# The last batch of a two-lane mixer kernel in 64-row halves, and the lower lane's products for u moved eight places later

## The chip, the cores and the metric

The kernel runs on one core of a Trainium2 chip. The metric is the device time of one execution in microseconds; of several runs the median counts. The arithmetic is float32 in the reference; the kernel carries each operand as a rounded float32r part ("hi") and the rest ("lo"), and multiplies the parts that matter.

## The reference

```python
def _attn_ref(x, weight_gen):          # x: 8 x 4096 x 192, weight_gen: 8 x 4096 x 8 heads x 7 taps
    w = softmax(weight_gen, axis=-1)
    ...                                # causal: seven rows of x, each head's 24 columns weighted by w
    return einsum('bshk,bskhg->bshg', w, x_unf).reshape(B, S, D)

def _moe_ref(x, w_tok1, w_tok2, w_ch1, w_ch2):
    xt = x.transpose(0, 2, 1)
    h = np.maximum(xt @ w_tok1, 0.0) @ w_tok2      # over the 4096 places: 4096 -> 256 -> 4096
    u = x + h.transpose(0, 2, 1)
    h2 = np.maximum(u @ w_ch1, 0.0) @ w_ch2        # over the 192 channels: 192 -> 1536 -> 192
    return u + h2
```

`reference` is `_moe_ref(_attn_ref(x, weight_gen), ...)`.

## The kernel before

Work goes by chunks of 512 places: eight batches of eight chunks, 64 chunks `g` = 0 to 63. Of each chunk the core computes:

- the attention sums (VectorE products `pr`, L278 and L292, summed into `xa` partly by accumulating DMAs of GpSimd), which run some eight chunks ahead,
- `token1`: 16 products per half into the bank pair `th`, which hold the running sum of a batch; ScalarE seeds the banks with the sum so far (`w<-h1s`, L609) and takes it out again (`h1s<-w`, L637),
- `token2`: u = x + h of the next chunk in the bank pair `up`; ScalarE seeds it with x (`w<-xb`, L664), then come ten products of 128 rows (six for bank 0, four for bank 1), or ten per half; `uf` takes it out (L683, L684, L688). Then `u_parts` (L691 to L728) makes `u_hi` and `u_lo`, the operands of the next chunk, in places that suit both halves: eight copies on ScalarE and two subtractions on VectorE,
- `channel1`: six blocks `p`, each of nine products per half into a tile `ph` of two banks (54 products per half), with `take_h` behind each block: ScalarE's relu (L799) and VectorE's rest (L800) into `h`; for blocks 4 and 5 in two steps each into `h_spare` (L792, L793),
- `channel2`: 60 products of 128 rows, or 60 per half, into the bank pair `acc`, which ScalarE seeds with u (L878); `store` turns the result (L887, L888 on VectorE), copies it to `out_tile` (L897 on ScalarE, twelve copies) and sends it out.

**Two ways to run a chunk.** In the plain way TensorE's products of `token2` and `channel2` take 128 rows of the array, and those of `channel1` come in pairs of 64 rows. `in_lanes` (L1558) says which chunks run in lanes instead: 16 to 54. There `chunk_in_lanes` (L1398) gives every product as two of 64 rows, the upper half (lane 0) and the lower half (lane 1). The two lanes work through their lists in different order, so that one lane can be in `channel2` while the other is in `token2` or `token1`. Two halves must not write one bank at once: a bank belongs to one lane until that lane's products for it are done; then a relay (a `nop` on VectorE or ScalarE, whichever the planner thinks is free earlier, L1389) hands it over.

**What sets the order.** The order is made when the program is written. A planner inside the kernel keeps estimated times of the engines (`at`, `on`), of the lanes (`lane_at`) and a cost per product (`SLOT`, 226.7 ns), and always writes down the product of the lane that would start first (`run_lanes`, L1370). Each engine then runs its queue in that order, TensorE one queue for both lanes. Other ScalarE and VectorE work (attention, stores, u's parts) is fitted in by `pump`.

**The lists of a chunk in lanes** are in `section` (L1463): `a` is `channel2` for bank 0 (36 products per lane), `c` the one for bank 1 (24), `u` is `token2` (ten); `la`, `lc`, `lu` are the lower lane's. `early` and `late` are `token1`'s products; a chunk in lanes has the late ones, the first chunk has both. The upper lane runs a, u, c, then token1; the lower lane runs part of `lc`, then `lu`, the rest of `lc`, token1, `la`:

```python
upper = a + u + [hook(end_two), *c, late[0], hook(lambda: end_one("late"))]
lower = lc[:4] + lu + lc[4:14] + [hook(lambda: seed_late(1))] + lc[14:] + [late[1]] + la
```

`hook` marks a place where something is written down without a product: `end_two` the taking out of u and its parts, `seed_late` the seed of `th`. Three tiles of two banks (`ring`) serve `ph`, `up` and `th` in turn; block 3's `ph` gets the tile of block 0, `up` the one of block 3.

Of the kernel before, what the change touches and what calls it, by code (L numbers as in the profile page):

```python
# [22 lines left out]
def mixer_kernel(ctx: ExitStack, tc: tile.TileContext, x, wg, wt1, wt2, wc1, wc2, out):  # L23
# [629 lines left out]
    def token2(m, up=None, lists=None):  # L653
# [28 lines left out]
        if seeded:  # L682
            nc.scalar.copy(u[c, 1, :], up[e, 1, :])  # L683
            nc.scalar.copy(u[:, 0, :], up[:, 0, :])  # L684
        else:
            nc.vector.tensor_add(u[:, 0, :], up[:, 0, :], xb[:, 0, :])
            nc.vector.tensor_add(u[c, 1, :], up[e, 1, :], xb[e, 1, :])
        nc.vector.tensor_add(u[c, 1, :], up[c, 1, :], u[c, 1, :])  # L688

    def u_parts(m):  # L690
# [37 lines left out]
        return first(), second()  # L728

# [313 lines left out]
    HANDOVER = 60  # L1043
# [312 lines left out]
    def lane_start(s):  # L1356

        while lanes[s] and lanes[s][0][0] == 0:
            at["pe"] = max(at["pe"], lane_at[s]) if s == 0 else at["pe"]
            lanes[s].popleft()[2]()  # L1360
        if not lanes[s]:
            return None
        bank, t = lanes[s][0][1], lane_at[s]
        if bank in owner and owner[bank] != s:
            if bank not in turn:
                return None
            t = max(t, turn[bank][1] + HANDOVER)
        return t

    def run_lanes(until):  # L1370

        while True:
# [7 lines left out]
            if bank is not None:  # L1380
# [4 lines left out]
                else:  # L1385
                    count[bank] = count.get(bank, 0) + 1
                    if count[bank] == ITEMS[bank[:2]]:
                        by, eng = min((("dve", nc.vector), ("act", nc.scalar)), key=lambda x: at[x[0]])
                        relay = eng.nop(nofuse=True)  # L1389
                        behind(relay, ins)  # L1390
                        turn[bank] = relay, on(by, 60, lane_at[s] + HOP)
# [7 lines left out]
    def chunk_in_lanes(g):  # L1399
# [4 lines left out]
        twice = max(state["token1"], state["open"]) < g + NCH  # L1404
# [62 lines left out]
        def section():  # L1467
# [5 lines left out]
            if "early" in box:  # L1473
                early = [hook(lambda s=s: open_one("early", s)) for s in range(2)]
                upper = [early[0]] + a + u + [hook(end_two)] + c + [late[0]]
                lower = lc[:8] + [early[1], hook(lambda: end_one("early"))] + lu + lc[8:] + la \
                    + [hook(finish), late[1], hook(lambda: end_one("late"))]
            elif box["late"]:
                upper = a + u + [hook(end_two), *c, late[0], hook(lambda: end_one("late"))]
                lower = lc[:4] + lu + lc[4:14] + [hook(lambda: seed_late(1))] + lc[14:] + [late[1]] + la  # L1480
            else:
                upper = a + u + [hook(end_two)] + c
                lower = lc[:4] + lu + lc[4:] + la
# [36 lines left out]
        def end_two():  # L1520
# [3 lines left out]
            t = max(on("dve", 690, on("act", 620, t)), on("act", 620))  # L1524
            w_at.append(t)
            chains[3:3] = [Chain(items, t, ("u", m)) for items in u_parts(m)]
# [31 lines left out]
    def in_lanes(g):  # L1558

        return 2 * NCH <= g < NG - NCH - 1 and (ring or state["token1"] >= g + NCH - 1 and state["done"] > g + NCH)  # L1560
# [124 lines left out]
```

## Time and profile before

| | |
|---|---|
| median of three runs | 2068.48 us (2068.37 to 2068.87) |
| the profiled execution's own time | 2068.67 us |
| its span, first to last instruction | 2066.9 us |
| PE, PEld busy | 2033.7 us (98%), 1737.9 us (84%) |
| DVE, ACT busy | 1501.7 us (73%), 1449.3 us (70%) |
| granted TensorE clock | 1.00 of 2.4 GHz, mean of the span |

PE is TensorE's products, PEld its weight loads, which run beside them; DVE is VectorE, ACT is ScalarE, ACTq and DVEq are their queues' own steps. A product's record lasts longer than the step from one product to the next, because products are pipelined: busy time says little on the steps, starts say more. "64*128" in an instruction's form is a product on half of the array's rows. In lanes two products start in each step of about 0.227 us. The name `w` in rows of chunks in lanes is any tile of the ring: `w<-u_hi,w_hi` is `channel1`, `w<-w,h` is `token2`, `w<-xh,w` is `token1`. Until chunk 15 the program runs the plain way, to about 586 us; then lanes to 1805 us; then the plain way again.

### The profile page before, as it was taken

The numbers are of one execution on the slowest core, as the hardware profiler recorded it, in microseconds if no ns is written. First come the engines' busy times: TensorE is split into PE (matmuls) and PEld (weight loads), VectorE is DVE, ScalarE is ACT, GpSimd is POOL, SyncE is SP. The second block draws the span as 40 slices with busy tenths as digits, with TensorE's granted clock in tenths as the row PEclk, the third lists the DMA queues.
The fourth block names the chain that finished last, engine by engine and source line by source line (L and its number), as shares of the span: only waits on it lengthen the run. The fifth ranks groups of instructions, "written<-read, shape, count | busy, mean of one in ns | idle before, by whom it ended". The sixth has DMA issues, their size and how long they took to land.

```text
span 2066.9 us, 39312 instructions
## 1 busy us (share of the span) xinstructions
PE 2033.7 (98%) x16201; PEld 1737.9 (84%) x16201; DVE 1501.7 (73%) x1813; ACT 1449.3 (70%) x2360; POOL 210.6 (10%) x292
## 2 busy tenths in 40 slices
PE   7999999999999999999999999999999999999999
PEld 7878888888888888888888888888888889888887
DVE  9899888888987768777778777768778774343343
ACT  7887667677766676776766677667677667676665
POOL 1101111111111101101101110101100110000000
PEclk9999999999999999999999999999999999999999
DMA  9878778787886766766767666666666663222121
GB/s 337 276 228 230 198 210 230 210 237 199 231 220 174 194 173 167 192 180 171 191 160 197 182 169 185 176 174 190 179 172 181 173 160 117 72 68 62 51 64 24
DMA packets 180928, 361.93 MB, mean 175 GB/s; under 512 B 26138, under 2 KB 129178, under 8 KB 165004
## 3 DMA queue, kind: packets, MB, share of 16 engines
q1 hardware_dynamic: 145420, 225.35, 35.4%
q0 software_dynamic: 35328, 134.07, 27.8%
q8 instruction: 127, 2.08, 0.4%
q14 instruction: 53, 0.43, 0.1%
HBM read 222.77 MB, written 70.52 MB: 142 GB/s over the span
## 4 chain that ended last, share of the span: by engine, by line
PE 79%; DVE 14%; ACT 5%; issue 2%; ACTq 0%; DMA 0%; DVEq 0%
PE acc L469 22%; PE w L469 21%; PE acc L811 15%; PE ph L782 10%; DVE h L800 5%; PE w L782 5%; DVE pr L278 2%; PE up L676 2%; ACT h L799 2%; ACT w L664 2%; PE th L648 2%; DVE pr L292 1%; DVE prk L404 1%; DVE h_spare L793 1%; PE w L676 1%
## 5 line engine op out<-in xcount | busy, mean ns | idle before, releaser
L469 PE MATMUL acc<-h,w2s 64*128 64x512 f32 x3120 | 556.5, 388 | 0.0
L469 PEld LDWEIGHTS acc<-h,w2s 64*128 64x128 f32 x3120 | 441.3, 184 | 34.6
L469 PE MATMUL w<-u_hi,w_hi 64*128 64x512 f32 x1404 | 370.9, 389 | 0.0
L469 PE MATMUL w<-u_hi,w_lo 64*128 64x512 f32 x1404 | 368.7, 387 | 0.0
L469 PE MATMUL w<-u_lo,w_hi 64*128 64x512 f32 x1404 | 368.4, 386 | 0.0
L469 PE MATMUL acc<-h_spare,w2s 64*128 64x512 f32 x1560 | 335.6, 386 | 0.0
L811 PE MATMUL acc<-h,w2s 128*128 128x512 f32 x1400 | 325.6, 390 | 0.0
L799 ACT ACTIVATE h<-w 128x1024 fp32r<-128x1024 f32 x210 | 215.6, 1027 | 148.7 <-PE w L469 80.8
L278 DVE TENSOR_TENSOR pr<-xc,wg 128x768 f32<-128x768 f32 x336 | 313.0, 945 | 0.2
L811 PEld LDWEIGHTS acc<-h,w2s 128*128 128x128 f32 x1400 | 261.8, 188 | 54.4 <-issue 0.7
L800 DVE SCALAR_TENSOR_TENSOR h<-w,h 128x1024 fp32r<-128x1024 f32 x210 | 255.7, 1218 | 71.0 <-ACT h L799 70.5
L296 POOL DMA_DIRECT2D xa<-pr x168 | 146.7, 873 | 1374.2 <-DVE pr L292 1002.2
L469 PEld LDWEIGHTS acc<-h_spare,w2s 64*128 64x128 f32 x1560 | 258.4, 184 | 23.4
L469 PEld LDWEIGHTS w<-u_hi,w_hi 64*128 64x128 f32 x1404 | 250.8, 184 | 24.1 <-DVE h L800 2.9
L469 PEld LDWEIGHTS w<-u_hi,w_lo 64*128 64x128 f32 x1404 | 253.8, 184 | 20.0
L469 PEld LDWEIGHTS w<-u_lo,w_hi 64*128 64x128 f32 x1404 | 254.9, 184 | 17.0
L688 DVE TENSOR_TENSOR uf<-w,uf 64x512 f32<-64x512 f32 x47 | 32.1, 683 | 256.5 <-ACT uf L684 256.5
L897 ACT COPY out_tile<-oa 32x256 f32<-32x256 f32 x504 | 203.7, 404 | 7.6
L469 PE MATMUL w<-w,h 64*128 64x512 f32 x780 | 194.9, 393 | 11.0 <-ACT w L664 11.0
L469 PEld LDWEIGHTS w<-xh,w 64*128 64x128 f32 x1280 | 187.6, 186 | 6.6 <-ACTq L1389 0.8
L469 PE MATMUL w<-xh,w 64*128 64x384 f32 (+1 forms) x1280 | 192.2, 300 | 0.6 <-ACTq L1389 0.4
L469 PEld LDWEIGHTS w<-w,h 64*128 64x128 f32 x780 | 140.7, 184 | 40.3 <-ACT w L664 26.9
(147 smaller groups left out, 3192.3 us busy)
## 6 DMA issues: line engine op xcount, KB each, us to landing
w<-s SPq DMA_DIRECT2D x96, 1024.0 KB, 6.5
xa<-pr POOLq DMA_DIRECT2D x168, 384.0 KB, 4.9
xc<-in_x_dram POOLq DMA_DIRECT2D x42, 960.0 KB, 9.6
out_dram<-out_tile SPq DMA_DIRECT2D x128, 192.0 KB, 2.6
xb<-xs SPq DMA_DIRECT2D x348, 64.0 KB, 5.1
xs<-t SPq DMA_DIRECT2D x56, 384.0 KB, 3.3
raw<-in_moe_w_tok_dram SPq DMA_DIRECT2D x16, 1024.0 KB, 8.3
xc<-in_x_dram POOLq DMA_DIRECT2D x12, 840.0 KB, 10.5
```

What stands on the lines that cost most here:

```text
L278: nc.vector.tensor_mul(t.rearrange("p t (h g) -> p (t h) g", h=H).rearrange("p (o n) g -> p o n g", o=1), x_k, w)
L296: nc.gpsimd.dma_start(xat[m].rearrange("p t d -> p (t d)"), tap_sums[m].rearrange("p t d -> p (t d)"), accum_op=ALU.add)
L469: return lambda: nc.tensor.matmul(to, w, v, start=start, stop=stop, skip_group_check=True)
L648: nc.tensor.matmul(to, w[:, c, r * P:(r + 1) * P], xat[m][:, c, :], start=c == first, stop=c == last, skip_group_check=True)
L664: nc.scalar.copy(up.rearrange("p k (n b c) -> p (k n) c b", c=W, b=Q), xb.rearrange("p k (n c b) -> p (k n) c b", c=W, b=Q))
L676: nc.tensor.matmul(up[:, n, :], h1[:, k, d], w[:, l, k * N:(k + 1) * N], start=k == 0 and j == 0 and not seeded, stop=k == KR - 1 and j == ...
L688: nc.vector.tensor_add(u[c, 1, :], up[c, 1, :], u[c, 1, :])
L782: nc.tensor.matmul(ph[:, j, :], w[rows, k, p * P:(p + 1) * P], u[rows, k], start=n == 0, stop=n == len(steps) - 1)
L799: nc.scalar.activation(h[:, :, 0, :], ph, AF.Relu)
L800: nc.vector.scalar_tensor_tensor(h[:, :, 1, :], ph, 0.0, h[:, :, 0, :].bitcast(F32), op0=ALU.max, op1=ALU.subtract)
L811: nc.tensor.matmul(acc[n], w2s[:, f, d], h[:, j, l, :], start=False, stop=f == NF - 1 and i == len(steps) - 1, skip_group_check=True)
L897: nc.scalar.copy(dst, src[to:to + Q].rearrange("p (n e d) -> p n e d", n=2, d=Q)[:, n])
```

## The change

1. `in_lanes` now holds for 16 to 62, so the eight chunks 55 to 62 run in lanes too; chunk 63 stays plain. `twice` is limited so that no token1 product is asked for that doesn't exist.
2. In all three kinds of chunk in lanes the lower lane runs twelve products of `lc` before `lu`; before it was four, and eight in the first chunk in lanes. The seeds of `token1` stand at other places in the lists.
3. For u of chunks 57 to 63, `quick_parts` replaces `u_parts`: u's taking out and its parts are written down at once, in one order, five casts and one copy on ScalarE, three casts, one copy, one addition and two subtractions on VectorE. `token2` puts u's first copy on VectorE there.
4. The planner's allowance for handing a bank over is 200 ns ahead of the relay, where 60 ns stood ahead of it (`HOP`) and 60 ns behind it (`HANDOVER`).

```diff
@@ -681,7 +681,7 @@
         c, e = slice(0, DC), slice(DC, P)
         if seeded:
             nc.scalar.copy(u[c, 1, :], up[e, 1, :])
-            nc.scalar.copy(u[:, 0, :], up[:, 0, :])
+            (nc.scalar.copy if m <= NG - NCH else nc.vector.tensor_copy)(u[:, 0, :], up[:, 0, :])
         else:
             nc.vector.tensor_add(u[:, 0, :], up[:, 0, :], xb[:, 0, :])
             nc.vector.tensor_add(u[c, 1, :], up[e, 1, :], xb[e, 1, :])
@@ -726,6 +726,40 @@
             yield "u", 620, lambda: act(hi[e, 2], uc[c])
             yield "n", 0, last
         return first(), second()
+
+
+    def quick_parts(m, t):
+
+        ua, uc = uft[m][:, 0, :], uft[m][:, 1, :]
+        c, e = slice(0, DC), slice(DC, P)
+        hi, lo = ut[m] = [late.tile([P, 3, N], F32R, tag=x, name=x) for x in ("u_hi", "u_lo")]
+        f, fh = lo.bitcast(F32), hi.bitcast(F32)
+
+        def act(to, of, *after):
+            nc.scalar.copy(to, of)
+            return on("act", 620, *after)
+
+        def copy(to, of, *after):
+            nc.vector.tensor_copy(to, of)
+            return on("dve", 420, *after)
+
+        def sub(to, of, less, *after):
+            nc.vector.tensor_sub(to, of, less)
+            return on("dve", 680, *after)
+        wide, narrow = on("dve", 620, t), on("act", 620, t)
+        narrow = on("dve", 690, narrow)
+        a = act(hi[:, 0], ua, wide)
+        b = act(hi[c, 2], uc[c], narrow)
+        la = sub(lo[:, 0], ua, fh[:, 0], a)
+        copy(hi[c, 1], fh[e, 0])
+        lb = sub(lo[c, 2], uc[c], fh[c, 2], b)
+        act(hi[e, 1], fh[c, 0])
+        copy(hi[e, 2], fh[c, 2])
+        act(lo[e, 1], f[c, 0], la)
+        copy(lo[c, 1], f[e, 0])
+        act(lo[e, 2], f[c, 2], lb)
+        free["u"] = max(at["act"], at["dve"]) + HOP
+        return narrow
 
 
     ht, acc_t = {}, {}
@@ -1040,7 +1074,7 @@
     AHEAD = 2
     MOVES = 2
     LANE_TIGHT = 600
-    HANDOVER = 60
+    HANDOVER = 200
     state = {"token1": NCH - 1, "token2": -1, "vals": 0, "few": 0, "few_t": 0, "late": False, "jobs": deque(),
              "summed": NCH - 1, "turned": FT - 1, "parts": NCH - 1, "kept": FT - 1, "stored": -1, "out": -1,
              "done": NCH - 1, "w1": NCH + 1, "channel1": 0, "rest": 0, "open": 0}
@@ -1364,7 +1398,7 @@
         if bank in owner and owner[bank] != s:
             if bank not in turn:
                 return None
-            t = max(t, turn[bank][1] + HANDOVER)
+            t = max(t, turn[bank][1])
         return t
 
     def run_lanes(until):
@@ -1388,7 +1422,7 @@
                         by, eng = min((("dve", nc.vector), ("act", nc.scalar)), key=lambda x: at[x[0]])
                         relay = eng.nop(nofuse=True)
                         behind(relay, ins)
-                        turn[bank] = relay, on(by, 60, lane_at[s] + HOP)
+                        turn[bank] = relay, on(by, 60, lane_at[s] + HANDOVER)
             if s == 0:
                 at["pe"] = lane_at[0]
 
@@ -1401,7 +1435,7 @@
         top, low = lanes
         phs, box = {}, {}
         need(lambda: g in ut)
-        twice = max(state["token1"], state["open"]) < g + NCH
+        twice = max(state["token1"], state["open"]) < min(g + NCH, NG - 1)
 
         def before(p):
             phs[p] = w_tile("ph")
@@ -1472,15 +1506,15 @@
             late = [hook(lambda s=s: open_one("late", s)) for s in range(2)]
             if "early" in box:
                 early = [hook(lambda s=s: open_one("early", s)) for s in range(2)]
-                upper = [early[0]] + a + u + [hook(end_two)] + c + [late[0]]
-                lower = lc[:8] + [early[1], hook(lambda: end_one("early"))] + lu + lc[8:] + la \
+                upper = [early[0]] + a + u + [hook(end_two)] + c[:12] + [hook(lambda: seed_late(0))] + c[12:] + [late[0]]
+                lower = lc[:12] + [early[1], hook(lambda: end_one("early"))] + lu + lc[12:] + la \
                     + [hook(finish), late[1], hook(lambda: end_one("late"))]
             elif box["late"]:
                 upper = a + u + [hook(end_two), *c, late[0], hook(lambda: end_one("late"))]
-                lower = lc[:4] + lu + lc[4:14] + [hook(lambda: seed_late(1))] + lc[14:] + [late[1]] + la
+                lower = lc[:12] + lu + lc[12:16] + [hook(lambda: seed_late(1))] + lc[16:] + [late[1]] + la
             else:
                 upper = a + u + [hook(end_two)] + c
-                lower = lc[:4] + lu + lc[4:] + la
+                lower = lc[:12] + lu + lc[12:] + la
             if not twice:
                 lower.append(hook(finish))
             box["end"] = lane_at[0] + sum(x[0] for x in upper) + (twice or box["late"]) * T1
@@ -1521,9 +1555,12 @@
             m, t = g + 1, max(lane_at) + HOP
             pump(t + SLACK_M, (), t + SLACK_A)
             next(box["two"], None)
-            t = max(on("dve", 690, on("act", 620, t)), on("act", 620))
-            w_at.append(t)
-            chains[3:3] = [Chain(items, t, ("u", m)) for items in u_parts(m)]
+            if m > NG - NCH:
+                w_at.append(quick_parts(m, t))
+            else:
+                t = max(on("dve", 690, on("act", 620, t)), on("act", 620))
+                w_at.append(t)
+                chains[3:3] = [Chain(items, t, ("u", m)) for items in u_parts(m)]
             state["token2"] = m
             if m + 2 < NG:
                 add_chain(iter([("gate", 0, lambda: state["kept"] >= m + 2 + (m + 1) % 2),
@@ -1557,7 +1594,7 @@
 
     def in_lanes(g):
 
-        return 2 * NCH <= g < NG - NCH - 1 and (ring or state["token1"] >= g + NCH - 1 and state["done"] > g + NCH)
+        return 2 * NCH <= g < NG - 1 and (ring or state["token1"] >= g + NCH - 1 and state["done"] > g + NCH)
 
     for g in range(NG):
         if in_lanes(g):
```

How the order moves. First, TensorE in chunk 41, from the end of `channel1` to the first product of `token2` (`w_5980<-w2,h1`). Rows of the lower lane here are those of `acc1` and `token2`, of the upper lane those of `acc0`; the numbers of `h` rise with the block. Before:

```order
L469 MATMUL w_5982<-u_lo_15713,w1_hi_71 128x512
L469 MATMUL acc0_15917<-h_15864,w2s_73 128x512
L469 MATMUL acc1_15918<-h_15864,w2s_73 128x512
L469 MATMUL acc0_15917<-h_15889,w2s_73 128x512
L469 MATMUL acc1_15918<-h_15864,w2s_73 128x512
L469 MATMUL acc0_15917<-h_15889,w2s_73 128x512
L469 MATMUL acc1_15918<-h_15864,w2s_73 128x512
L469 MATMUL acc0_15917<-h_15889,w2s_73 128x512
L469 MATMUL acc1_15918<-h_15864,w2s_73 128x512
L469 MATMUL acc0_15917<-h_15889,w2s_73 128x512
L469 MATMUL w_5980<-w2_15714,h1_15040 128x512
```

and in the changed kernel, from the lower lane's ninth product of bank 1:

```order
L469 MATMUL acc1_15919<-h_15915,w2s_73 128x512
L469 MATMUL acc0_15918<-h_15915,w2s_73 128x512
L469 MATMUL acc1_15919<-h_15915,w2s_73 128x512
L469 MATMUL acc0_15918<-h_15915,w2s_73 128x512
L469 MATMUL acc1_15919<-h_15915,w2s_73 128x512
L469 MATMUL acc0_15918<-h_15915,w2s_73 128x512
L469 MATMUL acc1_15919<-h_15915,w2s_73 128x512
L469 MATMUL acc0_15918<-h_15942,w2s_73 128x512
L469 MATMUL w_5980<-w2_15713,h1_15040 128x512
L469 MATMUL acc0_15918<-h_15942,w2s_73 128x512
```

Before, the first product of `token2` follows four products of the lower lane in bank 1, all of block 0; now it follows twelve, the last from block 2. The upper lane has gone on to block 3 by then, and stood at block 1 before.

Second, TensorE at the end of the same chunk, where the upper lane has begun `channel1` of the next one (`u_hi`, `u_lo`) and the lower lane ends its `channel2` (`acc0<-h_spare`). Before:

```order
L469 MATMUL acc0_15917<-h_spare_5979,w2s_73 128x512
L469 MATMUL w_5982<-u_hi_16098,w1_lo_72 128x512
L469 MATMUL acc0_15917<-h_spare_5979,w2s_73 128x512
L469 MATMUL w_5982<-u_hi_16098,w1_lo_72 128x512
L469 MATMUL acc0_15917<-h_spare_5979,w2s_73 128x512
L469 MATMUL w_5982<-u_hi_16098,w1_lo_72 128x512
L469 MATMUL w_5982<-u_hi_16098,w1_hi_71 128x512
L469 MATMUL w_5982<-u_lo_16099,w1_hi_71 128x512
L469 MATMUL w_5982<-u_hi_16098,w1_hi_71 128x512
```

and now:

```order
L469 MATMUL acc0_15918<-h_spare_5979,w2s_73 128x512
L469 MATMUL w_5982<-u_hi_16097,w1_lo_72 128x512
L469 MATMUL acc0_15918<-h_spare_5979,w2s_73 128x512
L469 MATMUL w_5982<-u_hi_16097,w1_lo_72 128x512
L469 MATMUL acc0_15918<-h_spare_5979,w2s_73 128x512
L469 MATMUL w_5982<-u_lo_16098,w1_hi_71 128x512
L469 MATMUL w_5982<-u_hi_16097,w1_hi_71 128x512
L469 MATMUL w_5982<-u_lo_16098,w1_hi_71 128x512
L469 MATMUL w_5982<-u_hi_16097,w1_hi_71 128x512
```

Behind the last row of `acc0` comes one more product of the upper lane, its sixth of the block before (`w1_lo`) and its seventh now (`u_lo`), and then the lower lane's first of `channel1`. The lower lane stands one product further behind the upper one, in this and the other chunks of the middle batches.

Third, VectorE in the last batch, for one u (of chunk 60 or so), from the relu's rest of the chunk to the next `store`. Before:

```order
L890 TENSOR_TENSOR oc<-oc 64x512
L800 SCALAR_TENSOR_TENSOR h<-w,h 128x2x512 x4
L688 TENSOR_TENSOR uf<-w,uf 64x512
L800 SCALAR_TENSOR_TENSOR h<-w,h 128x2x512
L714 TENSOR_TENSOR u_lo<-uf,u_hi 128x512
L715 TENSOR_TENSOR u_lo<-uf,u_hi 64x512
L800 SCALAR_TENSOR_TENSOR h<-w,h 128x2x512
L887 STREAM_TRANSPOSE oa<-acc_22484 128x512
```

and now:

```order
L834 SCALAR_TENSOR_TENSOR h<-w,h 128x2x512 x4
L827 SCALAR_TENSOR_TENSOR h_spare<-w,h_spare 128x512 x4
L684 COPY uf<-w 128x512
L688 TENSOR_TENSOR uf<-w,uf 64x512
L747 TENSOR_TENSOR u_lo<-uf,u_hi 128x512
L743 CAST u_hi<-u_hi 64x512
L747 TENSOR_TENSOR u_lo<-uf,u_hi 64x512
L743 CAST u_hi<-u_hi 64x512
L743 CAST u_lo<-u_lo 64x512
L921 STREAM_TRANSPOSE oa<-acc_22548 128x512
L922 STREAM_TRANSPOSE oc<-acc_22549 128x512
```

Before, two `take_h` steps of the chunk stand between u's steps, and ScalarE has eight of u's ten parts; now all of `take_h` is ahead of u, and five of the ten parts and the first copy of u are VectorE's.

On ScalarE and VectorE the order of chunks 17 to 53 is the same before and after, but for a swap of neighbours on each of the two engines in the first chunk in lanes and the relays' places.

## Rows read from the trace of the kernel before

**Rows 1.** Busy times of chunk 53: us, PE, PEld, DVE, ACT, POOL, clock, DMA.
```profile
1743.20:1773.90 30.70, 30.70 (x284) 27.33 (x282) 12.53 (x15) 21.50 (x36) 0.00 (x0) 1.00 0.31 95
```

**Rows 2.** Chain of waits, last batch: start us, us, what.
```profile
1876.26 2.51 PE w L676 x10
1878.78 13.60 PE acc L811 x60
1892.38 12.49 PE w L782 x108
```

**Rows 3.** Who TensorE waited for, whole run: total us, times, longest us.
```profile
PEld w L469 <- ACT w L664: 26.9, 38, 0.9
...
PEld w L469 <- DVE h L800: 2.9, 16, 0.2
...
PEld w L469 <- ACTq L1389: 0.8, 1, 0.8
...
PEld w L469 <- ACT w L609: 0.6, 1, 0.6
...
PE w L469 <- ACT w L664: 11.0, 35, 0.4
```

**Rows 4.** Timeline, seed and first token2 product, chunk 41: start, us, what [idle <-releaser].
```profile
1383.59 1.02 ACT L664 COPY w<-xb 128x1024 f32<-128x1024 f32 x1
...
1384.66 0.18 PEld L469 LDWEIGHTS w<-w,h 64*128 64x128 f32 x1 [0.82 <-ACT w L664]
1384.66 0.50 PE L469 MATMUL w<-w,h 64*128 64x512 f32 x1 [0.40 <-ACT w L664]
```

**Rows 5.** Timeline, the same place in chunk 54: a load, its product, token2's load.
```profile
1786.70 0.18 PEld L469 LDWEIGHTS w<-u_lo,w_hi 64*128 64x128 f32 x1
...
1786.92 0.39 PE L469 MATMUL w<-u_lo,w_hi 64*128 64x512 f32 x1
...
1788.45 0.18 PEld L469 LDWEIGHTS w<-w,h 64*128 64x128 f32 x1 [0.38 <-ACT w L664]
```

**Rows 6.** Timeline of VectorE: the turns that begin a chunk's store.
```profile
1371.10 0.72 DVE L887 STREAM_TRANSPOSE oa<-acc 128x512 f32<-128x512 f32 x1 [0.71 <-PE acc L469]
...
1433.47 0.72 DVE L887 STREAM_TRANSPOSE oa<-acc 128x512 f32<-128x512 f32 x1 [0.71 <-PE acc L469]
...
1775.33 0.72 DVE L887 STREAM_TRANSPOSE oa<-acc 128x512 f32<-128x512 f32 x1 [5.76 <-PE acc L469]
...
2035.48 0.72 DVE L887 STREAM_TRANSPOSE oa<-acc 128x512 f32<-128x512 f32 x1 [6.79 <-PE acc L811]
```

**Rows 7.** Timeline, token1's seed and first product (chunk 41); its products (chunk 54).
```profile
1389.87 0.80 ACT L609 COPY w<-h1s 128x768 f32<-128x768 f32 x1
...
1391.64 0.33 PE L469 MATMUL w<-xh,w 64*128 64x384 f32 x1
...
1795.39 0.33 PE L469 MATMUL w<-xh,w 64*128 64x384 f32 x1
...
1797.64 2.92 PE L469 MATMUL acc<-h,w2s 64*128 64x512 f32 x24
```

**Rows 8.** Timeline, a chunk with softmax steps: block 0's h, block 3's first load.
```profile
1343.35 1.21 DVE L800 SCALAR_TENSOR_TENSOR h<-w,h 128x1024 fp32r<-128x1024 f32 x1
...
1344.62 0.18 PEld L469 LDWEIGHTS w<-u_hi,w_hi 64*128 64x128 f32 x1 [0.18 <-DVE h L800]
```

**Rows 9.** Timeline, last batch: from pairs of 64 rows to products of 128.
```profile
1876.19 2.15 PEld L676 LDWEIGHTS w<-w,h 128*128 128x128 f32 x10 [0.35 <-issue]
```

**Rows 10.** Timeline of ScalarE: first and last of u's steps in chunk 41.
```profile
1393.25 0.58 ACT L683 COPY uf<-w 64x512 f32<-64x512 f32 x1 [2.58 <-PE w L469]
...
1398.99 0.62 ACT L718 CAST u_lo<-u_lo 64x512 fp32r<-64x512 f32 x1
```

**Rows 11.** A VectorE cast of 64x512, at L769: ns min/median/max, start us.
```profile
L769 DVE CAST u_lo<-u_lo x1: 421/421/421, 89.1 to 89.1; 64x512 fp32r<-64x512 f32 x1
```

**Rows 12.** Timeline of VectorE, chunk 42, behind the last take of h.
```profile
1418.39 1.81 DVE L278 TENSOR_TENSOR pr<-xc,wg 128x768 f32<-128x768 f32 x2
```

## The prediction

> **What bounds the kernel now.** I read the busy times first. TensorE's products cover all of a chunk's 30.70 us, VectorE is busy 12.53 us of it and ScalarE 21.50, and the granted clock is 1.00, the upper level of 2.4 GHz [rows 1]. So TensorE sets the time, and only idle steps of TensorE can be won; busy time hides them, since a product's record (0.39 us) is longer than the step of 0.227 us between products of one lane. The list of who waited for whom names the steps: the weight loads of lanes wait 26.9 us in 38 places for ScalarE's seed of `up`, 2.9 us in 16 places for VectorE's `h`, and twice in the first chunk in lanes [rows 3]. The chain shows the last batch: 2.51 + 13.60 + 12.49 = 28.60 us a chunk, all TensorE's [rows 2].
>
> **The wait for the seed of `up`.** In chunk 41 the seed ends at 1383.59 + 1.02 = 1384.61 and the first load of `token2` starts at 1384.66, after 0.82 us without one [rows 4]. What is lost is less: a load is normally 0.22 us ahead of its product (1786.70, 1786.92) [rows 5], whereas the late one starts with it and its product lasts 0.50 instead of 0.39, so the product comes 0.11 behind its load [rows 4]. The loss is the idle time less 0.11. Three of the 38 places (chunks 52 to 54, without attention work) idle 0.38 [rows 5], the other 35 share 26.9 - 3 x 0.38 = 25.8, or 0.736 each: (0.736 - 0.11) x 35 = 21.9 us. A second way: two chunks take 1433.47 - 1371.10 = 62.37 [rows 6], 31.18 each; chunk 53 takes 30.70 with 0.27 lost [rows 1, 5]; 31.18 - 30.43 = 0.75, of which some 0.07 is the wait for `h` (below): 0.68 x 35 = 23.8. I take 22.5. The lowest bound is TensorE's own idle record, 11.0 us [rows 3]; I don't use it, because the overlapping records hide part of each gap.
>
> The change puts eight more products of the lower lane ahead of `token2`: 8 x 0.227 = 1.81 us. In the order ScalarE and VectorE run the same steps as before in these chunks, so the seed stays where it is, 0.7 us late against a place that moves by 1.81: about 1.1 us early. The wait goes, **-22.5 us**, and in chunks 52 and 53 another 2 x 0.27 = **-0.5**.
>
> What is late next? `token1`'s seed ends at 1390.67 and its first product follows at 1391.64, 0.97 us later [rows 7]. The lower lane has 34 products ahead of it as before, so without the stall the product comes 0.72 earlier and 0.25 us is left: enough for a load 0.22 ahead. The cost is nothing, and where ScalarE were late, it would be a stall here. The steps behind `token2` (u's parts, `store`, VectorE's products) wait for TensorE and move with it.
>
> **The lower lane is one product further behind.** In 16 chunks (every second one, those with softmax steps) block 3's first load waits for VectorE's `h` of block 0: that ends at 1343.35 + 1.21 = 1344.56, the load starts at 1344.62, 0.18 late [rows 8]. VectorE's steps hang on the lower lane's end, block 3 of the upper lane doesn't; one product more between the lanes makes this load 0.227 later against its place. If both lanes lose it each time, 16 x 0.227 = 3.6 us. If the lanes slide against each other within the given order (an offset of up to one product is free, and the stall at `token2` no longer lines the lanes up again), it costs nothing. I take the middle, **+1.8**, and keep 0 and 3.6.
>
> **The first chunk in lanes** loses a load to a relay that stands behind ScalarE's `h_spare` (0.8 us) and one to `token1`'s seed (0.6) [rows 3]. The first is reached four products (0.9 us) later now, the second's seed stands three casts of 0.62 [rows 10] earlier: (0.8 - 0.11) + (0.6 - 0.11) = **-1.2**, bounds 0 and -1.2.
>
> **The last batch.** From the store of chunk 53 to that of chunk 62 it takes 2035.48 - 1775.33 = 260.15 us for nine chunks [rows 6]. It holds one start of the plain way with its waits, and in each plain chunk two changes between pairs of 64 rows and products of 128, where no load can be put ahead: 0.35 idle at one [rows 9], about 0.2 us lost. After the change chunk 54 takes 30.70 - 0.27 = 30.43. The chunks 55 to 62 do the same without `token1`, whose 16 products take 1797.64 - 1795.39 = 2.25 [rows 7]: 28.18 each, 225.4 for eight. Together 255.9; at the end of the lanes the lower one runs its last three or four products alone, about 0.4. So 256.3 against 260.15, **-3.9**.
>
> This holds if u is ready in time, for without `token1` only the upper lane's 24 products of bank 1 (5.4 us) lie between the end of `token2` and the next `channel1`. The old steps take 1398.99 + 0.62 - 1393.25 = 6.36 [rows 10]. The new ones: ScalarE one copy and five casts, 0.58 + 5 x 0.62 = 3.7; VectorE three casts at 0.42 [rows 11], an addition and two subtractions of about 0.68, and a copy of 128x512 out of the banks, which the trace doesn't show; the turn of the same size out of the banks takes 0.72 [rows 6], ScalarE's narrower copy 0.58 [rows 10], I take 0.65. That is 4.0; with the hand-overs between the two some 4.3 us, a us to spare. Chunk 55 keeps the old steps, but what ends last there is `u_lo`, six products later in use.
>
> **One rule against the change.** A load runs beside the products of both lanes: at 1786.70 a load starts, its product follows 0.22 later, and the product ahead of it is still running [rows 5]. The Trainium skill ("TensorE: Matmul & The Clock Gate", section "Part 3: Packing small matmuls — row/col tiling") says that a weight load overlaps running products only when the row group differs. By that rule a lane would pay each load of 0.18 us, in the last batch, for the 60 + 10 products of a chunk that were of 128 rows, 8 x 70 x 0.18 = 101 us more. The trace doesn't agree; the sum goes by the 30.70 of a chunk in lanes.
>
> **The sum.** -22.5 - 0.5 + 1.8 - 1.2 - 3.9 = -26.3. The profiled execution took 2068.67, so 2042.4; the median of the runs is 0.2 lower: **2042.2 us**.
>
> **Rivals.** (A) The lanes slide and block 3 waits no more: the 1.8 goes, and with it up to 2.2 of today's wait: 2038 to 2040.4. (B) `token1`'s seed takes the place: each 0.1 us over the 0.25 that is left costs 3.5 us in 35 chunks, and a late load 0.11 each. For it speaks that a relay stands ahead of the seed on ScalarE in half of these chunks; against it, that the relay's product ends 1.5 us before ScalarE gets there. 0.3 late gives (0.05 + 0.11) x 35 = 5.6, so 2048; 0.5 late 2055. (C) u is late in the last batch, as with the old steps' 6.36: about 0.9 x 7 = 6.4, 2048.6. (D) The change does not do what it says, ScalarE's seed of `up` follows `token2` and the wait stays: only the ends are won, 2068.5 - 3.9 - 0.2 = 2064.4. (E) Slower than before: the relay that hands the second bank of `up` to the upper lane now stands behind two of VectorE's products in 16 chunks, which end at 1418.39 + 1.81 = 1420.20 [rows 12]; the upper lane needs the bank 36 products after the section's start (1414.3), at 1422.5. VectorE 2.3 us late is the point from which TensorE waits, and 1.6 us more eats the 26 us: 5 us late gives 16 x 2.7 = 43, 2085. Against it: those products start without idle time here. (F) The page's rule on loads: 2042 + 101 = 2143.
>
> **How the numbers follow.** Forecast 0.60 (its own 2040.4 to 2046), A 0.13, B 0.11, C 0.08, D 0.04, E 0.03, F 0.01. A measurement of this kernel can tell some 0.2% (4 us) from no change. Faster by more: forecast, A, B, C, 0.92; within: D, 0.04; slower: E and F, 0.04. The range runs from below A, with the last of the small waits gone, to C and the half of B: 2037.5 to 2050.
>
> **What the changed profile should show.** No load waits for `w<-xb`; a chunk of the middle batches takes 30.4 to 30.6 us; loads waiting for `h` 0.2 to 0.4 in 16 places or none; the chunks 55 to 62 28.1 to 28.3 us; no load behind `w<-h1s`. A new releaser with some 35 entries would make B right; 29 us a chunk in the last batch C. The prediction is wrong in its main step if the wait for `w<-xb` stays.

## The result, and the profile after

The changed kernel takes 2041.97 us (median of four runs, 2041.88 to 2042.06) against 2068.43 (2068.24 to 2068.87) of the kernel before: a ratio of 0.9872, 95% interval 0.9855 to 0.9889, or 26.5 us less. The forecast was 2042.2. The profiled execution's span fell from 2066.9 to 2040.3 us.

From the page of the changed kernel, busy times of the whole span:

```profile
PE 2018.7 (99%) x16761; PEld 1756.4 (86%) x16761; DVE 1519.5 (74%) x1857; ACT 1436.1 (70%) x2348; POOL 210.2 (10%) x292
```

TensorE is still the bound. The list of who waited for whom in the changed kernel, the weight loads of lanes alone (total us, times, longest us), answers to [rows 3]; L834 is what was L800, L1423 what was L1389:

```profile
PEld w L469 <- DVE h L834: 7.5, 18, 0.6
...
PEld w L469 <- ACTq L1423: 0.8, 1, 0.8
...
PEld acc L469 <- DVEq L1423: 0.6, 1, 0.6
```

The 26.9 us behind ScalarE's seed of `up` are gone, and so is the 0.6 behind the seed of `token1`. The wait for VectorE's `h` has grown from 2.9 us in 16 places to 7.5 in 18 (the two new places, 0.57 and 0.28 us, lie in the first chunk in lanes), the relay of the first chunk stayed, and one wait for a relay on VectorE is new. The same places in the timeline (start us, us, what, idle before and releaser), in order of time:

```profile
1355.87 0.72 DVE L921 STREAM_TRANSPOSE oa<-acc 128x512 f32<-128x512 f32 x1 [0.73 <-PE acc L469]
...
1368.39 1.02 ACT L664 COPY w<-xb 128x1024 f32<-128x1024 f32 x1
...
1370.49 0.18 PEld L469 LDWEIGHTS w<-w,h 64*128 64x128 f32 x1
...
1389.24 0.62 DVE L240 TENSOR_REDUCE mx<-wg 128x64 f32<-128x448 f32 x1
...
1389.78 1.21 DVE L834 SCALAR_TENSOR_TENSOR h<-w,h 128x1024 fp32r<-128x1024 f32 x1
...
1391.04 0.18 PEld L469 LDWEIGHTS w<-u_hi,w_hi 64*128 64x128 f32 x1 [0.41 <-DVE h L834]
...
1417.07 0.72 DVE L921 STREAM_TRANSPOSE oa<-acc 128x512 f32<-128x512 f32 x1 [0.72 <-PE acc L469]
...
1435.87 0.80 ACT L609 COPY w<-h1s 128x768 f32<-128x768 f32 x1
...
1436.73 0.18 PEld L469 LDWEIGHTS w<-xh,w 64*128 64x128 f32 x1
...
1436.90 0.42 PE L469 MATMUL w<-xh,w 64*128 64x384 f32 x2
...
1831.73 0.18 PEld L469 LDWEIGHTS acc<-h,w2s 64*128 64x128 f32 x1 [0.56 <-DVEq L1423]
...
1896.49 0.72 DVE L921 STREAM_TRANSPOSE oa<-acc 128x512 f32<-128x512 f32 x1 [1.52 <-PE acc L469]
...
1918.34 0.58 ACT L683 COPY uf<-w 64x512 f32<-64x512 f32 x1 [3.55 <-PE w L469]
...
1922.67 0.42 DVE L743 CAST u_lo<-u_lo 64x512 fp32r<-64x512 f32 x1
...
1923.30 0.18 PEld L469 LDWEIGHTS w<-u_hi,w_hi 64*128 64x128 f32 x1
...
1924.62 0.72 DVE L921 STREAM_TRANSPOSE oa<-acc 128x512 f32<-128x512 f32 x1 [1.52 <-PE acc L469]
```

Read it by pairs. Two middle chunks take 1417.07 - 1355.87 = 61.20 us, where they took 62.37 [rows 6]. The seed of `up` ends at 1369.41 and `token2`'s first load follows 1.08 us later, without idle time. The seed of `token1` ends at 1436.67; its first load starts 0.06 later and its product at 1436.90, in step with the other lane: close behind the seed, but nothing is lost. Block 3's load waits 0.41 us for `h` (0.18 in [rows 8]), and that `h` stands behind a softmax reduction (L240) which ends after ScalarE's part. A chunk of the last batch takes 1924.62 - 1896.49 = 28.13 us, before 28.60 [rows 2].

The stores' first turns cut the run into stretches (us between turns):

| stretch, store to store | before | after | difference | forecast |
|---|---|---|---|---|
| chunk 15 to 17: first chunk in lanes, and one stall at token2 | 67.76 | 65.58 | -2.2 | -1.2 - 0.6 |
| 17 to 51: middle, with softmax steps | 1059.87 | 1040.05 | -19.8 | -21.9 + 1.8 |
| 51 to 53: middle, without | 61.40 | 60.93 | -0.5 | -0.5 |
| 53 to 62: chunk 54 and the last batch | 260.15 | 256.00 | -4.2 | -3.9 |

### The profile page after: what moved, and what is told of

The parts are those of the page before. It is cut to its first block, busy times and chain, and to the rows that moved or that the text cites. A ratio compares the mean times of both kernels' runs of the same rounds, so it can differ in the third digit from the quotient of the medians.

```text
span 2040.3 us, 40471 instructions
## 1 busy us (share of the span) xinstructions
PE 2018.7 (99%) x16761; PEld 1756.4 (86%) x16761; DVE 1519.5 (74%) x1857; ACT 1436.1 (70%) x2348; POOL 210.2 (10%) x292
## 4 chain that ended last, share of the span: by engine, by line
PE 94%; DVE 4%; ACT 1%; DMA 1%; issue 0%; ACTq 0%; DVEq 0%
PE w L469 36%; PE acc L469 33%; PE acc L845 9%; PE ph L816 9%; PE up L676 2%; PE th L648 2%; DVE prk L404 1%; PE w L816 1%; DMA out_dram<-out_tile 1%; PE up L845 1%; PE tapsum L414 1%; PE th L627 1%; DVE h L834 1%; DVE pr L278 0%; PE acc L882 0%; DVE val L202 0%
## 5 line engine op out<-in xcount | busy, mean ns | idle before, releaser
L469 PE MATMUL acc<-h,w2s 64*128 64x512 f32 x3760 | 615.6, 387 | 0.1
L469 PEld LDWEIGHTS acc<-h,w2s 64*128 64x128 f32 x3760 | 500.3, 184 | 47.2 <-DVEq L1423 0.6
L469 PE MATMUL w<-u_hi,w_hi 64*128 64x512 f32 x1692 | 441.4, 389 | 0.1
L469 PE MATMUL w<-u_hi,w_lo 64*128 64x512 f32 x1692 | 437.0, 388 | 0.0
L469 PE MATMUL w<-u_lo,w_hi 64*128 64x512 f32 x1692 | 434.7, 387 | 0.0
L469 PEld LDWEIGHTS w<-u_lo,w_hi 64*128 64x128 f32 x1692 | 306.5, 184 | 26.0
L834 DVE SCALAR_TENSOR_TENSOR h<-w,h 128x1024 fp32r<-128x1024 f32 x194 | 236.3, 1218 | 61.7 <-ACT h L833 61.1
L845 PE MATMUL acc<-h,w2s 128*128 128x512 f32 x920 | 215.6, 391 | 0.0
L826 ACT ACTIVATE h_spare<-w 128x512 fp32r<-128x512 f32 x188 | 112.5, 598 | 133.2 <-DVE h_spare L827 86.3
L845 PEld LDWEIGHTS acc<-h,w2s 128*128 128x128 f32 x920 | 171.7, 188 | 35.6 <-issue 0.4
L827 DVE SCALAR_TENSOR_TENSOR h_spare<-w,h_spare 128x512 fp32r<-128x512 f32 x188 | 129.0, 686 | 83.5 <-ACT h_spare L826 83.5
```

Of the source, the lines that this page charges most:

```text
L469: return lambda: nc.tensor.matmul(to, w, v, start=start, stop=stop, skip_group_check=True)
L826: nc.scalar.activation(h[:, 0, :], ph[:, j, :], AF.Relu)
L827: nc.vector.scalar_tensor_tensor(h[:, 1, :], ph[:, j, :], 0.0, h[:, 0, :].bitcast(F32), op0=ALU.max, op1=ALU.subtract)
L834: nc.vector.scalar_tensor_tensor(h[:, :, 1, :], ph, 0.0, h[:, :, 0, :].bitcast(F32), op0=ALU.max, op1=ALU.subtract)
L845: nc.tensor.matmul(acc[n], w2s[:, f, d], h[:, j, l, :], start=False, stop=f == NF - 1 and i == len(steps) - 1, skip_group_check=True)
```

## The experiments

Each was run beside the kernel before, and its difference is taken against the 2041.97 of the changed kernel; the kernel before took 2068.14 to 2068.82 on the chips used, so differences under about half a microsecond are not read. "Time lost" below is worked out from the traces: each product is given its undisturbed step (0.2267 us for a pair of half products of 512 columns), and what the starts fall behind at a place is added up. Such a sum over the middle chunks is good to a few tenths of a microsecond, depending on how many products around a stall are counted to it.

### How many products ahead of token2

```diff
-lower = lc[:12] + lu + lc[12:16] + [hook(lambda: seed_late(1))] + lc[16:] + [late[1]] + la
+lower = lc[:4] + lu + lc[4:14] + [hook(lambda: seed_late(1))] + lc[14:] + [late[1]] + la
```

and the same four in the list without `token1`; then six and eight (`lc[:6]`, `lc[:8]`) with the seed left at `lc[16:]`. VectorE and ScalarE run the same order in all of them.

> Four of the lower lane's products ahead of token2 again in the steady chunks and the last batch (the seeds of token1 at their old place); all else as in the changed kernel. Mine: the wait for the seed of up comes back, 35 x 0.63 = 21.9 us in chunks 17 to 51, and 0.27 in each of the 11 chunks without softmax work, 3.0: 2041.97 + 24.9 = 2066.9, with about 29 us of idle loads behind ScalarE's copy of x; the wait for h stays at its new 7.5 us, since the order still has the lower lane seven products behind. Rival (the lanes slide, and the stall lines them up again): the same stall, but the wait for h falls back to 2.9, 2064.5. If the gain came from the last batch or the first chunk, the time stays near 2042 to 2046.

> Six products ahead of token2 instead of twelve, nothing else. Mine (the seed's time is fixed by ScalarE, each product ahead is worth 0.227 us): idle 0.736 - 2 x 0.227 = 0.28 in 35 chunks, of which 0.17 is lost each: +6.0, so 2048.0; none in the chunks without softmax work. Rival (the seed moves with the place of token2, because ScalarE's copy hangs on something in the section): the wait hardly shrinks, 2060 or more.

> Eight products ahead of token2 instead of twelve, nothing else. Mine: the load comes 4 x 0.227 - 0.736 = 0.17 after the seed, no wait: 2042.0, within 0.5. Rival (the seed moves with the place): 2050 or more.

Measured: 2069.12 us with four (ratio to the kernel before 1.0005, 0.9996 to 1.0014), 2049.81 with six, 2041.99 with eight. The waits of TensorE's loads with four:

```profile
PEld w L469 <- ACT w L664: 26.3, 46, 0.7
...
PEld w L469 <- DVE h L834: 7.4, 18, 0.6
```

with six:

```profile
PEld w L469 <- DVE h L834: 7.5, 18, 0.6
PEld w L469 <- ACT w L664: 6.3, 31, 0.2
```

and with eight the first row is the same, and there is none for the seed:

```profile
PEld w L469 <- DVE h L834: 7.5, 18, 0.6
```

The longest wait goes from 0.7 to 0.2 to none, the mean one between chunks 17 and 51 from 0.64 to 0.20 to none: each product ahead is worth its 0.227 us, and the seed stays where it is. That is the main term of the prediction, and the rival in which the seed moves with `token2` is out. Eight would have done; the last four products buy nothing here. The rival that a stall lines the lanes up again is out too, since the wait for `h` stays at 7.4.

One thing went otherwise than I expected: with four the kernel is 2.2 us slower than I said, with six 1.8. With four, the time lost at `token2` between chunks 17 and 51 is 20.4 us, 2 less than in the kernel before. But each of the 16 late loads of block 3 loses 0.35 us in both runs, where it loses 0.29 in the changed kernel at the same order and the same idle record (0.41), and the many small losses grow as well. So a stall elsewhere makes the other one dearer; why, these runs don't settle. Without this part the whole change would have brought nothing: the stretches of chunks 15 to 17 and 54 to 63 gain 1.6 us each, and the middle one takes 4.0 more than in the kernel before, at the wait for `h` and in small losses.

### The last batch

```diff
-return 2 * NCH <= g < NG - 1 and (...)
+return 2 * NCH <= g < NG - NCH - 1 and (...)
```

> Chunks 55 to 62 the plain way again, all else as in the changed kernel. Mine: the last batch's term alone, 3.9 to 4.1 us: 2046.0. Rival (what the last batch gains is lost again at its ends, or the gain there comes from u's new steps rather than from the lanes): 2042 to 2043.

2045.96 us, 4.0 more. The loads of a plain chunk there, where half products and whole ones change places:

```profile
1853.33 2.15 PEld L676 LDWEIGHTS w<-w,h 128*128 128x128 f32 x10 [0.35 <-issue]
1869.45 0.53 PEld L816 LDWEIGHTS w<-u_hi,w_hi 64*128 64x128 f32 x6 [0.35 <-issue]
```

Two such changes a chunk, and nothing else idles: 28.60 - 28.13 = 0.47 us, some 0.23 each. In lanes they don't occur. The Trainium skill ("TensorEngine Tiling (Array Packing)", section "Key Properties") says that a change of the tiling mode drains TensorE; it gives no price. These rows agree with it as far as they go: the load is released by nothing but its own issue, and it starts together with its product, where a load within a stretch of one kind starts some 0.2 us ahead.

Then u's old steps in the last batch:

```diff
-if m > NG - NCH:
-    w_at.append(quick_parts(m, t))
+if False:
...
-(nc.scalar.copy if m <= NG - NCH else nc.vector.tensor_copy)(u[:, 0, :], up[:, 0, :])
+nc.scalar.copy(u[:, 0, :], up[:, 0, :])
```

> u's old steps (eight copies on ScalarE, two subtractions on VectorE, fitted in by the planner) in the last batch too, with its chunks in lanes. By my sum for rival C: 6.4 us of steps against 5.4 us of products that cover them, about 0.9 x 7 = 6.4 us more: 2048.4, and the loads of channel1 wait for u. Rival (the cover is longer than I counted, the new steps were not needed): 2042 to 2043.

2044.84 us: 2.9 more, neither of the two. 2.5 of it lie in the stretch of chunks 54 to 63 (250.48 for 248.00), and the list names no load there that waits for u. From the list of waits of this kernel:

```profile
PEld acc L469 <- DVEq L1423: 2.6, 7, 0.6
```

and from its timeline (chunk 57; the row at 1867.86 is the first product of chunk 58):

```profile
1855.38 0.69 DVE L827 SCALAR_TENSOR_TENSOR h_spare<-w,h_spare 128x512 fp32r<-128x512 f32 x1 [0.66 <-ACT h_spare L826]
...
1859.94 0.61 PE L469 MATMUL w<-w,h 64*128 64x512 f32 x2
1860.46 0.18 PEld L469 LDWEIGHTS acc<-h,w2s 64*128 64x128 f32 x1 [0.34 <-DVEq L1423]
...
1862.67 0.58 ACT L683 COPY uf<-w 64x512 f32<-64x512 f32 x1 [3.98 <-PE w L469]
...
1867.86 0.50 PE L469 MATMUL w<-u_hi,w_hi 64*128 64x512 f32 x1
...
1868.22 0.61 ACT L718 CAST u_lo<-u_lo 64x512 fp32r<-64x512 f32 x1
```

The old steps take 1862.67 to 1868.83, 6.16 us, near the 6.36 that I had, yet they cost far less than the sum for rival C: their last parts, `u_lo`, are used six products after `u_hi`. A chunk takes 28.55 us in place of 28.13, 0.42 more. About 0.3 of it is lost where the lower lane's first product in bank 0 of `acc` waits for a relay, though VectorE, which carries it, had been idle since 1856.07. The other 0.1 is lost where the upper lane's first product of `channel1` starts together with its load (1867.86), 0.8 us after the last part of `u_hi` was ready (1867.03).

Why the relay is late stays open. The lower lane reaches bank 0 after 24 + 10 products, the upper lane leaves it after 36, so a lower lane close behind has little time; by the order of the products the lower lane is three behind here and four in the changed kernel. But chunk 56 of the changed kernel waits 0.56 us (1831.73, above) with the lanes four apart, as in the chunks behind it, which lose nothing. What the chunks that lose time there have in common is when the relay runs: 0.07 to 0.15 us after the recorded end of the lower lane's own last product in bank 1, and 0.2 to 0.5 us after the recorded end of the upper lane's last product in bank 0; in chunk 57 of the changed kernel it runs 0.07 after the latter. Which engine carries the relay isn't it: with eight ahead ScalarE does so in chunk 56, and the load waits 0.54.

### The first chunk in lanes

```diff
-upper = [early[0]] + a + u + [hook(end_two)] + c[:12] + [hook(lambda: seed_late(0))] + c[12:] + [late[0]]
-lower = lc[:12] + [early[1], hook(lambda: end_one("early"))] + lu + lc[12:] + la \
+upper = [early[0]] + a + u + [hook(end_two)] + c + [late[0]]
+lower = lc[:8] + [early[1], hook(lambda: end_one("early"))] + lu + lc[8:] + la \
```

> The first chunk in lanes with its old lists (eight products ahead of token2, the seed of token1 at its old place), all else as in the changed kernel. By the prediction's term (idle loads alone): +1.2, so 2043.2. By the stretch of the two traces in which that chunk lies (67.8 us before, 65.6 after): +2.2, so 2044.2, since a lane that runs alone loses 0.11 us a product without any idle record. The lower lane stays seven products behind, so the wait for h is as it is.

2043.32 us, 1.35 more. Loads of the first chunk that waited, in this kernel:

```profile
601.90 0.18 PEld L469 LDWEIGHTS w<-xh,w 64*128 64x128 f32 x1 [0.78 <-ACTq L1423]
618.69 2.35 PEld L469 LDWEIGHTS w<-xh,w 64*128 64x128 f32 x22 [0.60 <-ACT w L609]
```

and from its list of waits:

```profile
PEld w L469 <- DVE h L834: 6.6, 16, 0.4
```

The wait for the seed is back. The relay's wait is the same with the new lists (0.8 in the first list above), so that one was never won. What was: 0.5 us at the seed, and the time around the two waits in which one lane runs alone. In this kernel six products ahead of the seed's wait (617.0 to 618.1) and five ahead of the relay's (600.2 to 601.2) stand alone, each 0.227 us behind the one before it, so that half of its step, 0.113 us, is lost; the changed kernel has two such products ahead of the relay, and loses 0.6 us around `token1`'s seed where this one loses 2.3. Against the gain stand the two loads of the first chunk that wait 0.57 and 0.28 us for `h` in the changed kernel, and don't here (16 places, not 18). The stretch of -2.2 also holds the first stall at `token2`, 0.7, which I hadn't taken out of it; the first chunk's own part is about -1.4.

### How near the seed of token1 is

```diff
-nc.scalar.copy(th[:, :, cols], h1s[b])
+[nc.scalar.copy(th[:, r, cols], h1s[b][:, r]) for r in ((1, 0) if lists is not None else ())] \
+    or nc.scalar.copy(th[:, :, cols], h1s[b])
```

> The seed of token1 in two copies of 128x384 in place of one of 128x768, the bank used first written last, in chunks in lanes; nothing else moves. The two should take some 0.25 us more than the one of 0.80. Rival B's price: the margin between the seed's end and its first product is 0.16 to 0.27 us in the changed kernel and no more is free, so 0.1 to 0.25 us lost in each of about 35 chunks: +4 to +9, 2046 to 2051, and a new releaser behind ScalarE's copy of h1s. If the margin is larger than it looks (the lanes slide): 2042.

2046.40 us, 4.4 more. From the timeline of this kernel:

```profile
1439.07 1.00 ACT L609 COPY w<-h1s 128x384 f32<-128x384 f32 x2
...
1440.12 0.18 PEld L469 LDWEIGHTS w<-xh,w 64*128 64x128 f32 x1 [0.15 <-ACT w L609]
1440.12 0.44 PE L469 MATMUL w<-xh,w 64*128 64x384 f32 x1
```

and from its list of waits:

```profile
PEld w L469 <- ACT w L609: 0.5, 3, 0.2
```

The seed takes 1.00 us in place of 0.80, its first load starts together with its product, and the stretch of chunks 17 to 51 takes 4.15 us more. In 30 of its 34 chunks the first load starts together with its product, and about 0.1 us is lost there each time; most of the rest is lost at block 3, which gets dearer again, as with four ahead. So 0.2 us more was already too much: rival B stood as near as the 0.25 us that the prediction left. The list of waits shows 0.5 us of the 4.4: a late load that starts with its product idles hardly longer than one that doesn't.

### Relays on VectorE

```diff
-by, eng = min((("dve", nc.vector), ("act", nc.scalar)), key=lambda x: at[x[0]])
+by, eng = ("dve", nc.vector)
```

> Every relay that hands a bank over on VectorE, whatever the planner thinks is free earlier. Mine: every hand-over but those of the first chunk has over 2 us to spare, so nothing or up to 1 us: 2042 to 2043. Rival E (VectorE's products ahead of a relay make it late): loads that wait for VectorE's queue in 16 or more chunks, some us up to 2085.

2043.49 us, 1.5 more, of which the stretch of chunks 15 to 17 has 66.75 - 65.58 = 1.2, where another order of TensorE came with it. The stretch of 17 to 51 takes 1040.15 (1040.05), and no load waits for a relay there. Rival E has no ground in this kernel.

### The lanes closer together

From chunk 18 on the upper lane is held back once by one, two or three products, so that the lower lane stands six, five or four behind it in place of seven:

```diff
-upper = a + u + [hook(end_two), *c, late[0], hook(lambda: end_one("late"))]
+upper = [hook(lambda: not_before(0, lane_at[0] + 1 * SLOT))] * (g == 18) + a + u + [hook(end_two), *c, late[0], hook(lambda: end_one("late"))]
```

with `2 * SLOT` and `3 * SLOT` in the other two.

> From chunk 18 on the lower lane stands six products behind the upper one, as before the change, in place of seven; VectorE's and ScalarE's order is the same. Mine (block 3's first load waits for VectorE's h of block 0, which hangs on the lower lane's end; each product between the lanes is 0.227 us): the loss there falls from 4.6 to some 2.2 us in 16 chunks, 2039.6. Rival (VectorE is late for a reason of its own, the reduction that stands ahead of that h, and moves with the upper lane): nothing, 2042.

> The lower lane five products behind from chunk 18 on. Mine: idle of 0.4 us at block 3's load less 2 x 0.227 is below nothing, the wait for h is gone: 2041.97 - 4.6 = 2037.4, below both kernels. Rivals: nothing changes, 2042; or a closer lower lane comes too early for a bank or a seed, a new wait eats the gain, over 2038.

> The lower lane four products behind from chunk 18 on. Mine: as with five, 2037.4, since no wait for h is left to win. Rival: the lower lane is early for something that the trace doesn't show yet, and the time rises again.

Measured: 2036.40, 2035.38 and 2035.45 us (ratios to the kernel before 0.9843, 0.9839 and 0.9840; the second's interval is 0.9822 to 0.9855). Waits for `h` with one product:

```profile
PEld w L469 <- DVE h L834: 4.0, 18, 0.6
```

with two:

```profile
PEld w L469 <- DVE h L834: 1.3, 3, 0.6
```

and the turns of the second kernel, two chunks apart:

```profile
1351.46 0.72 DVE L921 STREAM_TRANSPOSE oa<-acc 128x512 f32<-128x512 f32 x1 [0.34 <-PE acc L469]
...
1412.28 0.72 DVE L921 STREAM_TRANSPOSE oa<-acc 128x512 f32<-128x512 f32 x1 [0.37 <-PE acc L469]
```

The wait hangs on the distance of the lanes: a late load of block 3 idles 0.41 us with seven between the lanes, 0.18 with six, and with five it doesn't; the three waits that are left lie between 625 and 657 us, ahead of the place where the lane is held back. VectorE's reduction still stands ahead of that `h`, so the rival that VectorE is late whatever the lanes do is out. The gains are larger than I said: 5.6 us with one product, in place of 2.4, and 6.6 with two, in place of 4.6. The stretch of chunks 17 to 51 falls from 1040.05 to 1033.89 us with two. Of these 6.2 some 4.4 come from block 3's load in the 16 chunks with softmax steps. About 1.1 come from the same load in the chunks between, which I had left out: it is late by only 0.11 us there, too little for the list of waits, but the products behind it start 0.233 us apart in place of 0.227 for a while. Two chunks take 60.82 us, and 2 x (28.11 + 2.25) = 60.72 is what their products take without a stall, with 28.11 for a chunk of the last batch (next run) and 2.25 for `token1` [rows 7].

Last, five products and u of chunk 56 by the new steps too, so that the last batch's lanes start five apart:

```diff
-if m > NG - NCH:
+if m >= NG - NCH:
...
-(nc.scalar.copy if m <= NG - NCH else nc.vector.tensor_copy)(u[:, 0, :], up[:, 0, :])
+(nc.scalar.copy if m < NG - NCH else nc.vector.tensor_copy)(u[:, 0, :], up[:, 0, :])
```

> The lower lane five products behind from chunk 18 on (as in e10), and u of chunk 56 by the new steps too, so that the lanes of the last batch stand five products apart from its start. Mine: in the changed kernel chunk 55 loses 0.42 us where the lower lane's first product in bank 0 of the result waits for the relay, because its lanes stand only two products apart there; with five the upper lane is done with the bank earlier: 2035.38 - 0.4 = 2035.0, and no wait for a relay behind chunk 16. Rival (the relay itself is late on VectorE): the 0.4 stay, 2035.4.

2035.38 us (2035.08 to 2035.49; ratio 0.9840, 0.9826 to 0.9853). The turns of chunks 55 and 56:

```profile
1805.69 0.72 DVE L921 STREAM_TRANSPOSE oa<-acc 128x512 f32<-128x512 f32 x1 [1.69 <-PE acc L469]
1833.80 0.72 DVE L921 STREAM_TRANSPOSE oa<-acc 128x512 f32<-128x512 f32 x1 [1.69 <-PE acc L469]
```

28.11 us for chunk 56 (the expectation calls it 55), which took 1840.22 - 1811.67 = 28.55 in the changed kernel, and no load waits for a relay in the last batch. That the greater distance is what did it isn't shown, since u's steps moved too. The whole time doesn't show the 0.4, since the middle took 0.5 us more in this profile (1034.43 against 1033.89), for which I have no cause. The two kernels are one as far as time goes; both beat the changed kernel by 6.6 us.

The new allowance for hand-overs (200 ns) was not tried alone.

## Why the prediction was right, point by point

- **The wait for the seed of `up`** (-22.5): right in size and kind. The kernel before loses 22.4 us at `token2` between chunks 17 and 51, and 0.7 in the first; the changed one next to nothing. That the loss is the idle time less 0.11 holds, and that a product ahead is worth 0.227 us is shown by the four, six and eight. In chunks 52 and 53, without softmax work, the gain was 0.5, as forecast.
- **What is late next**: right, and close. The 0.25 us left for the seed of `token1` came out as a load 0.06 us behind the seed and 0.17 ahead of its product. With 0.2 us more it was late. Rival B was near, as its 0.11 said.
- **One product further behind** (+1.8, between 0 and 3.6): the lanes didn't slide. Time lost at block 3 went from 2.2 to 4.6, **+2.4**, about two thirds of 3.6. With the same load in the chunks between, which the term left out, it is about +3, so the term was too small. The mechanism holds: the idle time grew by 0.23 us, as one product more says. The middle between two ends was a guess and its nearness luck: on a single queue of TensorE a load that waits can hold both lanes, so there was little reason to count on sliding.
- **The first chunk** (-1.2): the sum was near the measured 1.4, and half its reason was wrong. The step that failed is "the first is reached four products (0.9 us) later now": the load that waits for the relay waits 0.8 us as before. The other part was larger than its idle time, because around a wait the other lane runs alone, 0.113 us lost on each product, and no view shows this as idle. That block 3's load would wait in this chunk too, and take some of the gain back, was left out.
- **The last batch** (-3.9): -4.2, with the store of chunk 62 at 256.00 us after that of 53 where the forecast had 256.3, and by the chunk lengths as forecast (28.13 for 28.18, and 0.42 lost in chunk 56, which I hadn't seen). 4.0 of it hang on the lanes, as their run alone shows; the stall of chunk 54 is the rest. That u's steps fit was right with less to spare than I said: 4.75 us (1918.34 to 1923.09) for my 4.3, with the first load 0.2 us behind the last of them. Rival C was wrong in its mechanism, as shown above: the old steps cost 0.42 us a chunk, about 0.3 of it at a relay, and not the 0.9 by which they were to be late (0.9 x 7 is 6.3, besides, not 6.4).
- **The rule on loads** (F): the trace speaks against it once more. The Trainium skill ("TensorE: Matmul & The Clock Gate", section "Part 3: Packing small matmuls — row/col tiling") lets a load overlap running products only in another row group; in the last batch all loads run beside products of the same half, and a chunk takes 28.13 us where undisturbed steps of the products alone give 28.11.

The terms' errors (-0.6, 0, +0.6, -0.2, -0.3) are small and partly cancel; the total of 26.5 against 26.3 is nearer than the terms deserve.

## What to carry to other kernels

Where a wait can't be made shorter, count by how much it is late and put that many products of the other kind ahead, and then look at who was late by less: here a distance of lanes that nobody had aimed at cost 6.6 us, and one held-back product in the plan removed most of it. Price a stall by where the starts fall behind, not by idle records: these show too much where loads run ahead, and too little where a lane runs alone or a load starts with its product.

## What the runs showed of the hardware

- A product that starts together with its load, because the load waited, takes 0.50 us in the record (1384.66, [rows 4]), and the next of its lane starts about 0.11 us later than its step.
- What a late load costs isn't its idle time alone. At an idle time of 0.41 us block 3's load lost 0.35 us in the runs with four and six ahead and 0.29 in the changed kernel; at 0.18 us it lost 0.15 in the kernel before, which had the stall at `token2`, and 0.05 with the lanes one product closer, without that stall.
- In the changed kernel the first loads of `token1` start 0.11 to 0.22 us ahead of their products, and the late end of that range loses no more than the early one: waiting until then costs nothing, however close it looks. At 0.00, in the run with the longer seed, some 0.1 us is lost.
- A change between half products and whole ones costs about 0.23 us, with 0.35 us of idle load and no releaser but issue.
- Half a step, 0.113 us, is lost on each product that a lane runs while the other waits (617.0 to 618.1, in the run with the old first chunk).
- A bank handed over through an engine that has nothing else to do: from the start of the first lane's last product in the bank to the second lane's load it took 0.52 us in the changed kernel (1859.29 to 1859.81, chunk 57, nothing lost) and 0.75 in the run with u's old steps (1859.71 to 1860.46). A relay has a price even where nobody is busy.
